# RWKV-style block on one core: the sums of the present token's part as column tiles of 64 tokens, and a new order of all engines

## The chip, the cores and the metric

One NeuronCore of one Trainium2 chip runs the whole program. The metric is the device time of one execution in microseconds; the kernel before was run three times, and their median is 341.69 us (340.33 to 343.31). The core has five engines that read their own instruction streams: TensorE (PE in the profile, PEld for its weight loads), VectorE (DVE), ScalarE (ACT), GpSimd (POOL) and SyncE (SP, which here issues all DMAs).

## The reference

Three layers follow one another, in float32, for 2 batches, 768 tokens and 384 = 8 x 48 channels:

```
for t in range(S):                                   # a linear attention with decay, per head (48 x 48 state)
    cur = einsum('bhd,bhe->bhde', u * k_t, v_t)
    y[t] = einsum('bhd,bhde->bhe', r_t, state + cur)
    state = w_t[..., None] * state + einsum('bhd,bhe->bhde', k_t, v_t)
h = gelu(x @ w_in); u, v = halves of h               # x is y, w_in 384 x 1024
v_s = w_sg @ layernorm(v) + b_sg                     # w_sg 768 x 768, over the tokens
x = x + (u * v_s) @ w_out
k = relu(mix(x, x_prev, mu_k) @ w_k) ** 2            # w_k 384 x 1024
out = sigmoid(mix(x, x_prev, mu_r) @ w_r) * (k @ w_v)
```

The part of `y[t]` that comes from `cur` is the present token's part: the number `sum_d r[t,d] u[d] k[t,d]` of each head and token, times `v_t`. The change concerns how TensorE forms this number.

## The kernel before

**The work.** Tokens are taken in four groups g of 384 (two batches, two halves), each in three chunks of 128. The attention is done in 16 units: unit i is one group and one pair of heads (p = 0 to 3), units 0 to 3 belong to group 0, 4 to 7 to group 1, and so on. The heads of a pair lie on partitions 0 to 47 and 64 to 111. The channels of r, k and w come in 12 packs (three for each group), pack j of a group holding pair j; the rows 48 to 63 and 112 to 127 of the three packs hold pair 3, and small DMAs (`move`) collect these into the tile `six`. The fifth to eighth layer steps use matrices of 64-bit input that DVE and ACT first turn into pairs of float32r (high and low part); each product of two such pairs is three TensorE products.

**The order.** Nothing is scheduled by a planner at run time. The string ORDER is read token by token, each token calls one method, and each engine keeps its instructions in the order in which the tokens stand. An engine that waits holds everything behind it. The tokens that matter here:

- for a pack: `L` load of the decays, `q` load of r and k, `D`, `j`, `g` the decay products and their inverses (DVE), `d` their product with r and k (DVE), `K` the product r x k that the sums read (DVE), `f` a range test (ACT), `6` the `move`;
- for a unit: `A` scores (TensorE, six products into the PSUM tile `pA`), `P` sums (TensorE, also into `pA`), `T` and `k` the turned keys (TensorE, ACT), `S`, `s`, `x` the states of the three chunks (TensorE, TensorE, ACT), `m` the mask on the scores and `n` the product of the sums with v (both DVE, both reading `pA`), `J`, `N`, `I` the output products (TensorE), `O` and `o` the copy and, for p = 3, the DMAs that share its rows out into `xT` (ACT, SP);
- for the layers: `C` with a number, the pieces of weights (`l` load, `x`, `b`, `t`, `o` on DVE, `h`, `r`, `q` on ACT); `X` the split of `xT` (ACT `h`, DVE `l`); `v`, `u` the products with w_in; `M` those with w_sg; `G`, `W` the gate and w_out; `H`, `Y`, `E`, `R`, `Z`, `z`, `y` the last layer;
- `e` a product that nobody reads (line 620), 128 x 512 in bfloat16, which keeps TensorE at work; `Q` the load of the constants; `|` the point where the attention's memory goes to the second half of the work.

A token such as `v0.2` or `M1.3` that stands several times runs one further step of the same piece of work each time: its first place is TensorE's.

**Rings that order the work.** `pA` has one buffer: the scores of a unit wait until `m` and `n` of the unit before have read it. The results of `v`, `u`, `M`, `W` and `E` take turns in three PSUM buffers (`ps_d`), so that the fourth of them waits until ACT or DVE has read the first. `wt` and `rk` have two buffers each. The pair that w_out is cast into lies in memory that the attention has until its last share DMA has landed.

**The lines that the change touches.** `sums` (line 319 on) is six products of a unit, each a chunk and a head: 48 rows, 128 tokens as the weights, and one moving column, a column of u. They write one column for each chunk into each of the two banks of `pA`, and `now` (line 361 on) reads them from there. The scores (line 317) have weights of the same 48 x 128 shape; the states (lines 334 and 345) have weights of 64 or 48 columns at column 0 or 64 of the array.

Of the kernel before, what the change touches and what calls it, by code (L numbers as in the profile page):

```python
# [36 lines left out]
ORDER = """e e L0 e q0 D0 j0 g0 f0 d0 e e e e e e e e e e e e e e e e e e e Q K0 A0 P0 L1 w0 q1 L2 D1 n0 j1 m0 g1 e e T0 e e e k0 S0.0 S0.1 J0 x0.0 s0.1 S0.2  # L37
x0.1 e N0 f1 s0.2 I0 x0.2 D2 d1 j2 K1 g2 A1 P1 w1 q2 C0.l m1 d2 n1 L3 K2 C0.x D3 T1 e e e e e f2 k1 S1.0 S1.1 x1.0 J1 s1.1 S1.2 A2 P2 x1.1 s1.2 x1.2
O0 e N1 T2 e I1 60 61 w2 L4 k2 S2.0 S2.1 O1 x2.0 m2 C0.b n2 j3 D4 g3 j4 62 A3 P3 q3 w3 q4 C1.l C0.t m3 g4 n3 s2.1 S2.2 J2 x2.1 s2.2 x2.2 e e T3 N2 J3
k3 C0.h S3.0 S3.1 e x3.0 N3 s3.1 S3.2 I2 K3 C0.o d3 C1.x x3.1 f3 I3 O3 s3.2 C1.r x3.2 f4 O2 C2.l w4 d4 C1.b A4 P4 m4 w5 L5 C2.x n4 e e T4 k4 C1.q e e  # L40
e S4.0 s4.0 S4.1 J4 o3 o3 o3 x4.0 s4.1 C1.t C1.h x4.1 K4 C2.b A5 P5 T5 N4 I4 k5 X0.2.h D5 C2.t X0.1.h S5.0 s5.0 S5.1 C2.h C2.r j5 X0.2.l C1.o C2.o e
v0.2 x5.0 X0.0.h C2.q C0.r s5.1 g5 X0.0.l C0.q x5.1 v0.0 q5 C3.l w6 C4.l 64 C5.l 63 C3.x d5 C3.b X0.1.l T6 v0.1 C3.t K5 65 m5 O4 k6 v0.0 f5 C3.h C3.r
C4.x n5 C3.o S6.0 s6.0 S6.1 J5 N5 I5 x6.0 C3.q s6.1 x6.1 C5.x C4.b C5.b C4.t C5.t A7 P7 T7 C4.h C4.o C5.h v0.2 C5.r L7 L6 C5.o u0.3 q6 w7 C11.l O5
u0.3 C11.h k7 D6 u0.2 u0.1 j6 g6 f6 m7 n7 A6 P6 d6 C11.o m6 n6 D7 K6 v0.2 v0.0 S7.0 s7.0 S7.1 J7 x7.0 s7.1 x7.1 J6 T8 N6 N7 A8 P8 I7 I6 q7 L8 C9.l w8
C7.l w9 j7 g7 m8 q8 D8 n8 j8 K8 d7 K7 g8 d8 v0.0 u0.1 k8 C5.q S8.0 S8.1 O7 v0.0 x8.0 O6 o7 o7 o7 J8 s8.1 S8.2 u0.0 C4.r f7 v0.1 x8.1 N8 I8 s8.2 C9.h
x8.2 A9 P9 u0.2 X1.1.h T9 X1.1.l m9 C7.h C7.o n9 C9.o X1.2.h X1.0.h X1.0.l k9 v1.1 S9.0 S9.1 x9.0 J9 s9.1 S9.2 A10 P10 x9.1 s9.2 v0.2 O8 u0.0 q11
C17.l C17.h L9 D9 X1.2.l v0.0 j9 g9 w10 68 v1.1 x9.2 f8 u1.2 v1.2 m10 T10 N9 v1.0 v0.1 v1.1 k10 v0.2 v0.2 v0.1 u1.2 w11 C6.l q9 66 d9 K9 L10 C8.l C8.h
C8.o n10 S10.0 S10.1 x10.0 f9 J10 s10.1 S10.2 I9 x10.1 s10.2 x10.2 67 A11 P11 T11 u1.1 N10 L11 C12.l q10 v1.2 O9 k11 v1.1 S11.0 S11.1 C6.h v0.1 x11.0
v1.1 C17.o D10 j10 m11 g10 n11 v0.1 C6.o d10 J11 s11.1 S11.2 A12 P12 x11.1 s11.2 C15.l D11 j11 g11 d11 C15.h x11.2 v1.0 u1.3 T12 u1.0 N11 I11 I10 v1.0
v1.2 C10.l w12 n12 m12 K10 C10.h C15.o v1.1 A13 P13 v1.0 C12.h B w13 n13 C10.o K11 m13 O11 k12 S12.0 s12.0 S12.1 u1.3 v1.0 v1.0 x12.0 u1.0 v1.2 u1.1  # L50
v1.2 J12 s12.1 o11 O10 o11 o11 C14.l C4.q x12.1 v1.2 M0.1 M0.3 T13 M0.3 C12.o M0.3 N12 M0.0 X2.1.h f11 C14.h k13 X2.1.l M0.1 M0.0 C13.l C13.h C14.o
C13.o M0.1 v2.1 S13.0 s13.0 S13.1 J13 x13.0 s13.1 x13.1 C16.l C16.h X2.2.h A14 P14 611 w14 69 C21.l X2.2.l C16.o w15 C18.l 610 N13 T14 M1.3 M0.0 C21.x
C21.b n14 C21.t m14 I13 I12 A15 P15 C20.l C21.r n15 M1.3 C20.x M1.3 m15 C26.l k14 v2.1 v2.1 v2.1 O13 S14.0 s14.0 S14.1 C21.q x14.0 J14 s14.1 x14.1
X2.0.h X2.0.l v2.2 T15 M1.0 O12 C26.r M1.0 C20.b C20.t k15 v2.2 C26.q S15.0 s15.0 S15.1 x15.0 J15 s15.1 v2.2 f10 v2.2 x15.1 C20.r C20.q N15 N14 M1.1
I14 I15 C19.l O15 o15 o15 C18.r O14 o15 | C20.h C21.h C18.q G0.3.h M1.0 M1.1 v2.0 C20.o C19.x C21.o C18.x C19.b C18.b G0.3.l C19.t M0.2 M1.2 v2.0
C19.r v2.0 C19.h v2.0 v2.0 v2.1 v2.2 M0.2 C19.o C26.x M0.2 C26.b C26.t v2.0 M1.2 v2.1 G0.0.h C19.q G0.2.h u2.0 u2.0 u2.3 u2.2 u2.1 v2.2 M1.1 C23.l
C27.l G0.1.h u2.3 G0.2.l G0.0.l C18.t C18.h C23.r C26.h G0.1.l C18.o C22.l u2.1 X3.0.h u2.2 X3.1.h X3.2.h W0.1 C23.x M1.2 C23.b X3.0.l C26.o C22.x
X3.2.l C22.b W0.1 C22.t X3.1.l C23.t W0.2 W0.2 W0.0 W0.0 C22.h C23.h C23.o C34.l v3.0 v3.0 v3.0 v3.1 v3.1 C23.q v3.0 C34.x C22.o v3.2 u3.2 v3.1 u3.1
v3.2 v3.2 v3.0 u3.2 u3.1 v3.2 u3.3 u3.0 C34.b C34.t v3.0 v3.2 v3.1 v3.1 v3.1 v3.2 C27.x C27.b C27.t G1.3.h u3.0 G1.0.h u3.3 C27.r C27.q C34.h M2.2
M3.1 M2.1 C27.h G1.2.h C34.r C34.q G1.1.h M2.2 G1.0.l C22.r C22.q G1.3.l G1.2.l C27.o C34.o G1.1.l C24.l M3.1 C24.x C24.b C24.r C24.t C24.q M2.2 W1.0  # L60
M2.1 C35.l C25.l C25.x C25.b C35.r C24.h C35.q C25.r C37.l C24.o W1.0 C35.x C35.b C35.t C35.h C25.q W1.1 M2.0 C38.l W1.1 C25.t C25.h C25.o C38.x M2.1
C37.r M2.3 M2.3 M2.3 M3.1 C35.o M2.0 W1.2 G2.1.h C37.q G2.2.h C37.x G2.1.l M2.0 G2.2.l C37.b W1.2 G2.3.h G2.0.h M3.2 M3.3 M3.0 M3.2 C37.t C38.b G2.3.l
M3.2 G2.0.l C38.t M3.3 C36.l C28.l W2.0 H0 Y0.0.0.a Y0.0.2.a Y0.0.0.b Y0.0.0.c Y0.0.1.a Y0.1.0.a Y0.1.1.a C36.r C37.h Y0.1.0.b Y0.1.1.b C36.q M3.0
M3.0 C37.o Y0.0.1.b C28.x W2.0 C38.h Y0.0.2.b C28.b W2.2 W2.1 C38.r C38.q Y0.0.2.c Y0.0.1.c Y0.1.0.c W2.1 Y0.1.2.a M3.3 E0.0 Y0.1.2.b E0.0 E0.2 E0.2
C28.r C38.o C36.x C36.b C28.t E0.0 E0.2 C36.t W2.2 Y0.1.1.c E0.1 E0.4 G3.0.h C28.h E0.0 E0.2 C36.h E0.2 C28.q E0.1 Y0.1.2.c C36.o C30.l C29.l C31.l
E0.5 R0.0 E0.3 R0.1 E0.0 C29.x C29.b C28.o E0.1 E0.1 E0.5 C31.x C31.b C29.t C29.h R0.0 G3.1.h E0.1 H1 C29.o C30.x G3.2.h C29.r C29.q E0.4 C30.b E0.5
C30.t C30.r C31.t Y1.0.0.a Y1.1.0.a C31.h Z0.0 E0.6 E0.5 C30.h Y1.0.1.a C30.o C32.l C32.x C31.o E0.5 C33.l E0.3 E0.4 E0.3 E0.4 E0.4 C32.b E0.3 C33.x
E0.3 C32.t C33.b C33.t C30.q E0.7 Z0.1 Z0.2 R0.2 C32.h E0.6 C32.o Y1.0.2.a E0.6 Y1.0.0.b E0.7 C31.r C33.h C33.o R0.2 E0.6 E0.7 E0.7 Y1.1.0.b Y1.0.1.b
Y1.1.1.a E0.6 Y1.1.1.b Y1.0.2.b R0.1 Y1.0.0.c E0.7 Z0.3 Z0.4 Z0.5 Z0.6 Y1.0.1.c Y1.0.2.c E1.1 Z0.7 Y1.1.2.a E1.1 Y1.1.2.b Y1.1.2.c E1.1 E1.0 E1.0 E1.0
# [826 lines left out]
```

## Time and profile before

| what | value |
|---|---|
| median of three runs | 341.69 us (340.33 to 343.31) |
| profiled execution | 341.91 us, span 340.1 us |
| PE busy, PEld busy | 330.4 us (97%), 306.2 us (90%) |
| DVE, ACT, POOL busy | 231.9 us (68%), 181.5 us (53%), 28.5 us (8%) |
| granted TensorE clock | 0.991 of full speed |
| chain that ended last | PE 80%, DVE 10%, ACT 5% |
| scores L317, sums L324 in that chain | 4%, 3% |

The busy times are shares of the span. A product is counted from its start to the end of its passage through the array, which is longer than the time until the next may start, so that a PE that is busy all the time is not a PE that starts something all the time; the distance between the starts of two weight loads says more. Instructions of DVE overlap a little as well: the next often starts some 80 ns before the one before it is over.

### The profile page before, as it was taken

The page shows a single profiled execution, that of the slowest core. Times are in us where ns is not written, and L with a number is a line of the kernel's source. Part 1 is how long each engine was busy: PE and PEld are TensorE (multiplying, and loading weights), DVE is VectorE, ACT ScalarE, POOL GpSimd, SP SyncE. Part 2 cuts the span into 40 slices and gives each one's busy share as a digit, 9 for nine tenths or more (in the row PEclk, how much of TensorE's full clock was granted, in tenths as well). Part 3 has the DMA queues.
Part 4 walks back from the last instruction along what each step waited for, and adds up shares of the span by engine and source line. Part 5 has one row for each costly group of instructions (what it writes and reads, how often), then busy time and mean ns, then how long its engine had stood idle before and what let it go on. Part 6 is the DMA issues. An engine that isn't in the chain of part 4 may idle for free.

```text
span 340.1 us, 6557 instructions
## 1 busy us (share of the span) xinstructions
PE 330.4 (97%) x2534; PEld 306.2 (90%) x2534; DVE 231.9 (68%) x427; ACT 181.5 (53%) x439; POOL 28.5 (8%) x74
## 2 busy tenths in 40 slices
...
GB/s 215 156 202 180 226 210 162 82 173 155 168 29 132 225 4 52 19 162 64 3 113 123 76 46 47 94 93 1 2 0 71 1 0 2 69 2 0 69 25 52
DMA packets 16500, 29.80 MB, mean 88 GB/s; under 512 B 2256, under 2 KB 12496, under 8 KB 16464
## 3 DMA queue, kind: packets, MB, share of 16 engines
...
q14 instruction: 15, 0.12, 0.1%
...
## 4 chain that ended last, share of the span: by engine, by line
PE 80%; DVE 10%; ACT 5%; issue 2%; DMA 1%; SPq 1%; POOL 1%; ACTq 0%; POOLq 0%; DVEq 0%
PE po L541 9%; PE pA L317 4%; PE idle L620 4%; PE pk L188 4%; PE pk L190 4%; PE pk L189 4%; PE ps L188 3%; PE ps L190 3%; PE ps L189 3%; PE py L374 3%; PE po L190 3%; PE po L188 3%; PE po L189 3%; PE py L384 3%; PE pv L188 3%; PE pA L324 3%
## 5 line engine op out<-in xcount | busy, mean ns | idle before, releaser
L188 PE MATMUL ps<-wsg,vn_hi 128*128 128x384 f32 x96 | 32.8, 342 | 0.0
L188 PE MATMUL pk<-xk_hi,wk_hi 128*128 128x384 f32 x96 | 32.5, 338 | 0.3 <-ACT kr L513 0.3
L190 PE MATMUL ps<-wsg,vn_lo 128*128 128x384 f32 x96 | 32.4, 337 | 0.0
L189 PE MATMUL ps<-wsg,vn_hi 128*128 128x384 f32 x96 | 32.4, 337 | 0.0
L189 PE MATMUL pk<-xk_lo,wk_hi 128*128 128x384 f32 x96 | 32.3, 337 | 0.0
L190 PE MATMUL pk<-xk_hi,wk_lo 128*128 128x384 f32 x96 | 32.3, 337 | 0.0
L513 ACT ACTIVATE kr<-pk 128x384 f32<-128x384 f32 x32 | 15.6, 489 | 29.9 <-PE pk L190 19.6
L515 DVE TENSOR_TENSOR kr<-kr 128x384 f32<-128x384 f32 x32 | 17.7, 555 | 14.0 <-ACT kr L513 14.0
L522 DVE TENSOR_TENSOR kk_lo<-kr,kk_hi 128x384 fp32r<-128x384 f32 x32 | 17.6, 554 | 13.2 <-ACT kk_hi L520 13.1
L520 ACT CAST kk_hi<-kr 128x384 fp32r<-128x384 f32 x32 | 16.1, 511 | 18.2 <-DVE kr L515 12.9
L541 PE MATMUL po<-pl_win_hi,kk_hi 128*128 128x384 f32 x81 | 23.0, 337 | 0.0
L188 PE MATMUL pu<-xs_hi,win_hi 128*128 128x384 f32 x48 | 16.9, 352 | 2.5 <-DVE sg L460 2.5
L460 DVE SCALAR_TENSOR_TENSOR sg<-ps,c_sb,bsg_bc 128x384 f32<-128x384 f32 x16 | 9.8, 614 | 13.9 <-PE ps L190 13.8
L541 PE MATMUL po<-pl_win_lo,kk_hi 128*128 128x384 f32 x63 | 18.5, 340 | 0.2 <-DVE pl_win_lo L169 0.2
L188 PEld LDWEIGHTS pk<-xk_hi,wk_hi 128*128 128x128 f32 x96 | 18.0, 188 | 0.6 <-ACT kr L513 0.6
L541 PE MATMUL po<-pl_win_hi,kk_lo 128*128 128x384 f32 x54 | 18.3, 338 | 0.0
L188 PEld LDWEIGHTS ps<-wsg,vn_hi 128*128 128x128 f32 x96 | 18.0, 188 | 0.1
L189 PEld LDWEIGHTS ps<-wsg,vn_hi 128*128 128x128 f32 x96 | 18.0, 188 | 0.0
L190 PEld LDWEIGHTS pk<-xk_hi,wk_lo 128*128 128x128 f32 x96 | 18.0, 188 | 0.0
L190 PEld LDWEIGHTS ps<-wsg,vn_lo 128*128 128x128 f32 x96 | 18.0, 188 | 0.0
L189 PEld LDWEIGHTS pk<-xk_lo,wk_hi 128*128 128x128 f32 x96 | 18.0, 188 | 0.0
L358 DVE TENSOR_TENSOR am<-pA,c_sb 128x768 f32<-128x768 f32 x16 | 15.2, 950 | 2.9 <-PE pA L324 2.9
...
## 6 DMA issues: line engine op xcount, KB each, us to landing
...
```

Of the source, the lines that this page charges most:

```text
L188: T.matmul(ps, lh, rh, start=(i == 0), stop=False)
L189: T.matmul(ps, lh, rl, start=False, stop=False)
L190: T.matmul(ps, ll, rh, start=False, stop=(i == n - 1))
L317: T.matmul(u.pA[:, h, c * C:(c + 1) * C], u.kinv[o:o + D, c, :], u.rp[o:o + D, c, :], start=True, stop=True)
L324: T.matmul(u.pA[:, h, TB + c:TB + c + 1], u.home()[o:o + D, 2 * WL + c * C:2 * WL + (c + 1) * C], c_sb[o:o + D, CU + u.p:CU + u.p + 1], st ...
L358: V.tensor_mul(u.am.rearrange("p h (c t) -> p h c t", c=NCB), u.pA[:, :, :TB].rearrange("p h (c t) -> p h c t", c=NCB), mask[:, None, None ...
L513: A.activation(kr, ps, AF.Relu)
L515: V.tensor_mul(kr, kr, kr)
L520: A.copy(hi, kr)
L522: V.tensor_sub(lo, kr, hi.bitcast(F32))
L541: T.matmul(pv[g][s], l, wv[i][r], start=st, stop=(i == KF - 1 and l is ll))
L620: T.matmul(ps_d.tile([P, 512], F32, name="idle", tag="d"), d[:, :P], d[:, :512], start=True, stop=True)
```

## The change

The sums take another shape. Each product still reads one chunk, but now half of its tokens (64 columns of the weights, at column 0 and at column 64 of the array), over all 112 rows of the two heads, and moves two columns: u of the first head and u of the second, each zero on the other head's rows. The result is one column for each head, in the first bank alone. The number of products stays at six. The two columns of the four pairs are made once, by four products on POOL behind the load of the constants. `now` reads the six columns from where they are.

The order of all engines is new; the multiset of tokens is the same, 1250 of them and 44 `e`. Ahead of the first unit stood 22 unread products and stand 19; 8 stand behind its sums, where 2 stood.

```diff
-ORDER = """e e L0 e q0 D0 j0 g0 f0 d0 e e e e e e e e e e e e e e e e e e e Q K0 A0 P0 L1 w0 q1 L2 D1 n0 j1 m0 g1 e e T0 e e e k0 S0.0 S0.1 J0 x0.0 s0.1 S0.2
...
-v0.2 x5.0 X0.0.h C2.q C0.r s5.1 g5 X0.0.l C0.q x5.1 v0.0 q5 C3.l w6 C4.l 64 C5.l 63 C3.x d5 C3.b X0.1.l T6 v0.1 C3.t K5 65 m5 O4 k6 v0.0 f5 C3.h C3.r
...
-C7.l w9 j7 g7 m8 q8 D8 n8 j8 K8 d7 K7 g8 d8 v0.0 u0.1 k8 C5.q S8.0 S8.1 O7 v0.0 x8.0 O6 o7 o7 o7 J8 s8.1 S8.2 u0.0 C4.r f7 v0.1 x8.1 N8 I8 s8.2 C9.h
-x8.2 A9 P9 u0.2 X1.1.h T9 X1.1.l m9 C7.h C7.o n9 C9.o X1.2.h X1.0.h X1.0.l k9 v1.1 S9.0 S9.1 x9.0 J9 s9.1 S9.2 A10 P10 x9.1 s9.2 v0.2 O8 u0.0 q11
...
+ORDER = """e e L0 D0 j0 g0 f0 e L1 D1 e e e e q0 K0 d0 e e e e e e e e Q q1 w0 j1 g1 d1 K1 e e e e T0 k0 A0 S0.0 S0.1 P0 e e e e e e e e f1 x0.0 n0 m0 A1 s0.1 P1
+S0.2 w1 L2 q2 J0 x0.1 s0.2 e e e x0.2 D2 j2 g2 m1 n1 d2 C1.l C1.x T1 k1 e e N0 S1.0 S1.1 x1.0 A2 s1.1 S1.2 J1 f2 x1.1 s1.2 x1.2 L3 K2 D3 P2 C1.b C0.l
...
+C5.q j7 g7 d7 K7 m8 J6 S8.1 N6 I6 L8 v0.2 f7 u0.1 x8.0 n8 A9 s8.1 S8.2 J8 x8.1 s8.2 P9 o7 q8 w9 C9.o D8 j8 g8 m9 K8 n9 x8.2 u0.3 d8 L9 O6 v0.0 v0.2
+v0.2 v0.0 C6.o C10.h D9 K9 u0.0 u0.2 o7 66 o7 f8 X1.0.h X1.0.l T9 A10 k9 S9.0 S9.1 x9.0 w10 C12.l C12.h J9 P10 s9.1 S9.2 N9 N8 x9.1 u0.2 v0.1 s9.2 I8
+I9 X1.1.h x9.2 C14.l B C12.o m10 j9 v1.0 C14.h u0.0 X1.2.h O8 g9 X1.1.l C10.o T10 k10 C14.o X1.2.l v1.2 u1.1 w11 q10 68 n10 C11.l 67 S10.0 S10.1 J10
...
+S15.1 J15 C15.h C15.o M0.2 n15 M0.2 x15.0 C21.r s15.1 x15.1 N15 I15 I14 C26.l C18.l v2.0 C21.q C19.r C19.q O15 O14 v2.2 o15 o15 o15 | C18.r C21.h
+C18.q C20.h v2.2 v2.0 C21.o v2.1 M1.1 C18.x C18.b C20.o C26.x C26.b M1.1 M1.1 C18.t v2.2 C18.h C18.o C19.x C19.b C26.t M0.1 C19.t M1.0 v2.0 v2.1 v2.1
+M1.0 M1.3 C26.h C26.o M1.3 M1.0 C19.h M1.2 M1.2 C19.o C23.l C22.l C26.r v2.1 G0.3.h C22.x C23.x u2.3 C26.q v2.0 v2.2 v2.2 v2.0 u2.3 v2.1 G0.1.h C22.b
...
+    uu = [ap1.tile([R, 2], F32, name=f"uu{p}") for p in range(NP)]
...
         def sums(u):
 
             for c in range(NCB):
-                for h in range(2):
-                    o = 64 * h
-                    T.matmul(u.pA[:, h, TB + c:TB + c + 1], u.home()[o:o + D, 2 * WL + c * C:2 * WL + (c + 1) * C],
-                             c_sb[o:o + D, CU + u.p:CU + u.p + 1], start=True, stop=True)
+                k = u.home()[:, 2 * WL + c * C:2 * WL + (c + 1) * C]
+                for o in (0, 64):
+                    T.matmul(u.pA[o:o + 64, 0, TB + 2 * c:TB + 2 * c + 2], k[:, o:o + 64], uu[u.p], start=True, stop=True)
...
-                         u.pA[:, :, TB:TB + NCB].rearrange("p h c -> p c h")[:, :, :, None].broadcast_to([P, NCB, 2, D]),
+                         u.pA[:, 0, TB:TB + 2 * NCB].rearrange("p (c h) -> p c h", c=NCB)[:, :, :, None].broadcast_to([P, NCB, 2, D]),
...
             nc.sync.dma_start(c_sb, cst)
+            for p in range(NP):
+                G.tensor_scalar_mul(uu[p], c_sb[:R, CB:CB + R:64], c_sb[:R, CU + p:CU + p + 1])
             G.tensor_scalar_mul(g_sb, g_sb, float(DH) ** 1.5)
```

## Rows read from the trace of the kernel before

**Rows 1.** Busy times by stretch: us, PE, PEld, DVE, ACT, POOL, PEclk, DMA.

```profile
8.72:65.38 56.66, 56.66 (x716) 47.28 (x715) 51.05 (x85) 35.26 (x94) 4.98 (x11) 1.00 0.62 179
...
152.00:335.30 183.30, 182.79 (x1033) 180.49 (x1033) 123.48 (x239) 90.14 (x204) 9.37 (x15) 1.00 0.14 45
```

**Rows 2.** Timeline of weight loads, scores, sums, states: start us, us, engine, line.

```profile
53.88 0.75 PEld L317 LDWEIGHTS pA<-pk 48*128 48x128 f32 x12 [0.25 <-issue]
54.55 0.75 PEld L324 LDWEIGHTS pA<-c_sb,pk 48*128 48x128 f32 x12
55.31 0.19 PEld L334 LDWEIGHTS pkv<-vk,kT 128*64 128x64 f32 x4
```

**Rows 3.** Timeline of weight loads, narrow groups of the states.

```profile
17.30 0.31 PEld L334 LDWEIGHTS pkv<-vk,kT 128*64 128x64 f32 x8 [0.42 <-ACT kT L310]
...
19.99 0.19 PEld L345 LDWEIGHTS pkv<-sx,c_sb 112*64 112x64 f32 x4
...
72.52 0.25 PEld L334 LDWEIGHTS pkv<-vk,kT 128*48 128x48 f32 x4
```

**Rows 4.** Timeline of weight loads, full-width loads behind column tiles.

```profile
57.24 0.30 PEld L306 LDWEIGHTS ptr<-c_sb,pk 112*128 112x128 f32 x3 [0.17 <-issue]
```

**Rows 5.** Timeline of the start, unread products and DVE's first wait for sums.

```profile
1.44 7.35 PE L620 MATMUL idle<-d1pat 128*128 128x512 bf16 x22 [1.44 <-POOL lim_tanh L119]
...
10.28 0.46 DVE L364 TENSOR_TENSOR vg<-pA,vk 128x288 f32<-128x288 f32 x1 [2.40 <-PE pA L324]
```

**Rows 6.** Groups of DVE by shape: busy us, mean ns, idle before.

```profile
L246 DVE TENSOR_TENSOR_SCAN pk<-wt,d1pat 128x387 f32<-128x387 f32 x12 | 11.4, 952 | 3.5 <-POOL xT L225 2.4 <-DMA wt<-in_wp_dram 1.1
L257 DVE TENSOR_TENSOR pk<-pk,rk 128x768 f32<-128x768 f32 x12 | 11.4, 952 | 0.1
...
L261 DVE TENSOR_TENSOR pk<-rk 128x384 f32<-128x384 f32 x12 | 6.6, 547 | 0.0
...
L169 DVE TENSOR_TENSOR wsg<-wsg_raw,wsg 128x384 fp32r<-128x384 f32 x12 | 6.5, 548 | 0.0
```

**Rows 7.** Timeline: DVE's `n8`, and the scores of unit 9.

```profile
61.63 0.43 DVE L364 TENSOR_TENSOR vg<-pA,vk 128x288 f32<-128x288 f32 x1
...
65.38 0.75 PEld L317 LDWEIGHTS pA<-pk 48*128 48x128 f32 x12
```

**Rows 8.** Timeline of weight loads: one `J`, one `u`, one `N`, one `I`.

```profile
61.40 0.68 PEld L374 LDWEIGHTS py<-am,vk 128*48 128x48 f32 x12
...
62.47 0.19 PEld L188 LDWEIGHTS pu<-xs_hi,win_hi 128*128 128x128 f32 x1
...
63.97 0.42 PEld L378 LDWEIGHTS py<-c_sb,vg 128*112 128x112 f32 x3
...
64.57 0.39 PEld L384 LDWEIGHTS py<-pk,sx 48*48 48x48 f32 x8 [0.17 <-issue]
```

**Rows 9.** Weight loads around two `v` groups, and one stretch's busy times.

```profile
67.72 0.21 PEld L188 LDWEIGHTS pv<-win_hi,xs_hi 128*128 128x128 f32 x1 [0.61 <-ACT xs_hi L415]
...
71.57 0.31 PEld L334 LDWEIGHTS pkv<-vk,kT 128*64 128x64 f32 x8 [0.44 <-issue]
...
78.77 0.19 PEld L188 LDWEIGHTS pv<-win_hi,xs_hi 128*128 128x128 f32 x1
...
81.06 0.31 PEld L334 LDWEIGHTS pkv<-vk,kT 128*64 128x64 f32 x8 [0.37 <-ACT uT L451]
...
69.00:70.00 1.00, 1.00 (x4) 0.71 (x3) 1.00 (x4) 0.25 (x1) 0.00 (x0) 0.50 1.03 326
```

**Rows 10.** Timeline behind the last shares: TensorE's and ACT's waits.

```profile
132.36 0.46 PEld L384 LDWEIGHTS py<-six,sx 48*48 48x48 f32 x8
...
138.76 0.93 ACT L166 CAST wout_hi<-wout_x 128x384 fp32r<-128x384 f32 x2 [3.75 <-DMA xT<-t]
...
143.63 0.19 PEld L188 LDWEIGHTS pu<-xs_hi,win_hi 128*128 128x128 f32 x1 [0.67 <-DVE sg L460]
...
147.62 0.19 PEld L188 LDWEIGHTS pu<-xs_hi,win_hi 128*128 128x128 f32 x1 [2.46 <-DVE sg L460]
```

More of the change, by code (lines that the diff above doesn't have):

```diff
@@ L49 @@
[L49 to L68, printed above, removed]
@@ new lines @@
+61 60 w2 C0.x C0.b j3 m2 g3 q3 62 N1 e e T2 I0 L4 n2 C1.t K3 d3 D4 I1 k2 O0 S2.0 S2.1 x2.0 J2 s2.1 S2.2 A3 f3 x2.1 s2.2 C1.h x2.2 P3 e T3 e N2 e w3 q4
+k3 S3.0 S3.1 O1 x3.0 C1.r m3 n3 K4 j4 g4 d4 A4 s3.1 S3.2 J3 x3.1 s3.2 C1.q x3.2 P4 C3.l L5 w5 w4 m4 D5 C0.t n4 N3 e T4 e e C2.l I3 k4 O3 I2 S4.0 s4.0
+S4.1 J4 x4.0 s4.1 O2 x4.1 C0.r C0.q j5 C1.o g5 e e e e T5 N4 q5 C2.x C2.b C2.t d5 o3 o3 o3 k5 C2.r C0.h C0.o A5 S5.0 s5.0 S5.1 P5 I4 X0.2.h x5.0 s5.1
+X0.0.h C2.h O4 f4 x5.1 X0.2.l 64 C5.l w6 K5 63 65 C2.o v0.2 C3.x X0.0.l T6 v0.0 k6 C2.q C3.r X0.1.h C3.q n5 m5 C5.x C5.b A7 C5.t X0.1.l S6.0 s6.0 S6.1
```

48 lines of the change are left out of this document (30 added, 18 removed).

## The prediction, made before the changed kernel was run

> **What bounds the kernel now.** I read the busy times by stretch first. Up to 65 us TensorE and DVE both work nearly without a pause: DVE is busy 51.05 of 56.66 us there, and from 152 us on TensorE starts 1033 products in 183.3 us, 0.177 us each, while DVE has a third of its time free [rows 1]. So there are two regimes. Late, a microsecond taken out of TensorE's stream is a microsecond of the end. Early, each unit's scores wait for DVE's `m` and `n` of the unit before, because `pA` has one buffer, so that DVE's stream sets the pace and what TensorE saves turns into waiting. The reader is to see in the timeline that even there a few waits stand out: DVE idles 2.40 us for the first sums, since 22 unread products, 7.35 us of them, stand before the first scores [rows 5]; a `v` group at 67.7 us waits and then runs at half the granted clock [rows 9]; and behind the attention's last shares ACT is held for 3.75 us and TensorE later for 0.67 and 2.46 us [rows 10].
>
> **The sums.** A unit's scores and sums are twelve weight loads each (two for a product) of 128 columns, and twelve such loads take 0.75 us from the first start to the last end [rows 2]. The new sums are twelve loads of 64 columns at alternating column halves, the shape of the states: four of these take 0.19 us, eight take 0.31, so four more cost 0.12 [rows 2, 3], and twelve should take 0.31 + 0.12 = 0.43. That is 0.32 us less for a unit, 5.1 us for sixteen. The shape itself (112 rows, two moving columns) isn't in the trace. Its bounds: a group of four that took 0.25 us [rows 3] gives 0.75 for twelve, no gain at all; at the least twelve take what four take, 0.19, a gain of 0.56 for a unit. A loss I exclude only as far as no row has a narrow load slower than a wide one. I take 0.32, the rows that are nearest in shape.
>
> A narrow group behind a wide one of the same rows starts without idle time [rows 2], but a full-width group behind column tiles waited 0.17 us [rows 4]. The sums now change array shape between themselves and the scores, which they did not before. The Trainium skill, TensorEngine Tiling (Array Packing), section Key Properties, says that a change of tiling mode drains TensorE, which speaks against the new shape; in the new order, though, all sixteen sums stand beside a group of states or `J`, which have their mode, and I count 71 changes of mode in place of 77, so by that rule the sum would be about 6 x 0.17 = 1.0 us better. I leave this out of the sum, since not every change shows a wait.
>
> **The head, up to the scores of unit 9.** Unread products are 44 before and after, and all of them stand ahead of `A9` in both orders, so they cancel there. The start changes: three fewer stand ahead of the first unit, and DVE is given `j1 g1 d1 K1` before it must wait for the first sums. I therefore take its 2.40 us of idling as gone. The second pack's load now stands ahead of the first `rk` and of the constants on SP, which delays these by one issue; DVE has `D1` to do meanwhile, so nothing. The four POOL products stand ahead of the gain's, long before the first sums: nothing. If SP or POOL were late after all, the first unit pays it once.
>
> In the new order `A9` stands right behind `n8`. Up to `n8`, DVE has the same instructions in both orders but for two: `d7` and `K7` have come in, `D8` and `C11.o` have gone out, 0.952 + 0.547 against 0.952 + 0.548 [rows 6]. So I put the new `n8` at the old one's end, 61.63 + 0.43 = 62.06, less 2.40: 59.7 us. The old scores of unit 9 start at 65.38 [rows 7]. The new ones come 5.7 us earlier, but with less done. By counting tokens, TensorE has put behind `A9` two `u` groups (1.50 each, from the first load to the next group's), `J8` (0.68), `N8` (0.42), `I8` (0.39) and three state groups (some 0.13 each): 4.9 us [rows 8]. The nine sums ahead of `A9` bring nothing of their own, as DVE sets that point. The seven behind it bring 7 x 0.32 = 2.2. Head and sums: 5.7 - 4.9 + 2.2 = **3.0 us**. For DVE's other idle time in the head I assume what it was: 56.66 - 51.05 - 2.40 = 3.2 us [rows 1, 5].
>
> **The event at 67 us.** The `v` group there waited 0.61 us for `X1.1.h`, which ACT could not start before a share's DMA had landed, and then nine products took 3.85 us up to the next group, against 2.29 for the group at 78.77; the granted clock was 0.50, the lower of its two levels [rows 9]. Together 0.61 + 1.56 = 2.2 us. In the new order the first share is issued a whole unit earlier (`o7` behind `P9`, `X1.0.h` after `u0.0 u0.2 o7 66 o7`), and `T9 A10 S9 J9 P10` and more stand between the splits and `v1.0`. I take the wait and the slow stretch as gone: **2.2 us**; the ends are 0 and 2.2. What could take its place: `A9`, which by the above may make TensorE wait for DVE.
>
> **Behind the last shares.** The old outer products end at about 132.8 and ACT gets on at 138.76, 5.9 us later [rows 10]. The new order has three groups for TensorE in between, `v2.1`, `M1.1`, `M1.0`: 45 products, 8.4 us by 0.2 and 0.177 each (an estimate from the 9 products in about 2 us of [rows 9] and from [rows 1]). Then `M1.3` needs the PSUM buffer of `v2.1`, whose GELU is ACT's ninth instruction behind the held cast: eight instructions of some 0.7 us make 5.9 + 5.9 = 11.8. So TensorE waits about 3.4 us, against 0.67 + 2.46 = 3.1 before [rows 10]. I take this as equal, with ends of -3 and +3.
>
> **The last layer** keeps its work, and TensorE was full there [rows 1]. I cost its new order at nothing; the cover is DVE's free third, and a `kk` or conversion that comes late would cost TensorE directly.
>
> **Sum.** 3.0 + 2.2 + 0 = 5.2 us. The profiled execution took 341.91 (span 340.1 and 1.8 around it), 0.2 above the median of 341.69: 336.7 against the former, **336.5** against the median.
>
> **Rivals.** (1) *The clock event only moves.* TensorE waits for DVE at `A9` or `A10`, and another group behind such a wait runs at the lower level. For it: the wait before the old event was only 0.61 us. Against: many small groups fill that stretch. Then 2.2 are lost: 338.7. (2) *The sums are no cheaper*, the shape costs what the old one did, by the group of four in 0.25 us: 7 x 0.32 is lost, again 338.7. (3) *DVE and TensorE wait for each other in the head*: DVE comes to `m` with the scores not yet done, unit by unit, and nine times pays scores and sums, 0.67 + 0.43 = 1.1 us: +9.9, 346.4, slower. It decides at `n8`: each microsecond after 59.7 costs one, from 64.9 on nothing is gained, from 68.3 on the kernel is over 1% slower. For it: 25 unread products now stand among the units, where 22 stood, so the order expects waits there. Against: DVE has conversions between `A` and `m` of most units. (4) *DVE's remaining idle time in the head shrinks too*: up to 3.2 us more, 333.3.
>
> **How the numbers follow.** Forecast 0.48, (1) 0.15, (2) 0.08, (3) 0.12, (4) 0.17. What a measurement can tell from no change is about 1%, 3.4 us, so faster means under 338.3. The forecast's own scatter is some 3 us, by the two ends of the wait behind the shares, and puts 0.06 of its chance above that line; of (1), 0.03 falls under it. Faster 0.42 + 0.17 + 0.03 = 0.62, slower 0.12, the rest 0.26. The range runs from 331.0 (case 4 with a cheaper sum or a shorter wait at the shares: 333.3 - 2.3) to 341.5 (case 1 or 2 with a longer one: 338.7 + 2.8); it leaves out case 3 and the tails of the others.
>
> **What would show it.** The twelve loads of the sums on line 325 in about 0.43 us; no DVE wait of over a microsecond for the first sums; `n8` at about 59.7 and the scores of unit 9 right behind it; full granted clock between 60 and 75 us; one wait of about 3 us for TensorE some 8 us after the last outer products, and from there to the end the same 0.177 us for each product. The prediction is wrong if `n8` comes after 62, if the loads of the sums take over 0.6 us, if the clock falls somewhere in the head, or if the last layer shows waits of TensorE that add up to more than 2 us.

## The result and the profile after

The changed kernel took 338.6 us (median of 11 executions, 337.8 to 340.1) against 342.4 for the kernel before beside it: ratio 0.989, 95% interval 0.986 to 0.992, so about 3.7 us or 1.1% faster. Measured again with other kernels it was 338.8, ratio 0.991 (0.988 to 0.995). The forecast was 336.5, a gain of 5.2. The profiled execution has a span of 337.0 us (before 340.1). One execution further down, of the new sums in the old order, ran over 1% slower than the others of its kernel, at a lower granted clock, and its time and profile are not used.

The head first. Weight loads and VectorE's (DVE's) products of the kernel after, timeline: start us, us, engine, line.

```profile
10.26 0.45 DVE L364 TENSOR_TENSOR vg<-pA,vk 128x288 f32<-128x288 f32 x1
...
59.16 0.46 DVE L364 TENSOR_TENSOR vg<-pA,vk 128x288 f32<-128x288 f32 x1
...
59.84 0.75 PEld L318 LDWEIGHTS pA<-pk 48*128 48x128 f32 x12 [0.18 <-DVE vg L364]
...
91.73 0.43 PEld L325 LDWEIGHTS pA<-uu,pk 112*64 112x64 f32 x12
92.08 0.20 PEld L334 LDWEIGHTS pkv<-vk,kT 128*64 128x64 f32 x4
```

The twelve loads of the sums take 0.43 us and the next group starts 0.35 us after the first of them, where it was 0.76 [rows 2]. DVE's 2.40 us of waiting at 10 us are gone [rows 5]. `n8` ends at 59.62 instead of 62.06, and unit 9's scores start at 59.84 instead of 65.38 [rows 7].

Next the waits of TensorE and what holds them, kernel after, timeline of the weight loads, ScalarE (ACT) and SyncE's queue (SPq).

```profile
36.62 0.51 ACT L415 CAST xs_hi<-xT 128x384 fp32r<-128x384 f32 x1 [2.11 <-DMA xT<-t]
37.39 0.19 PEld L345 LDWEIGHTS pkv<-sx,c_sb 112*64 112x64 f32 x4 [2.26 <-ACT sx L353]
...
61.95 1.22 SPq L273 DMA_DIRECT2D six<-pk  x2
63.28 1.31 SPq L395 DMA_DIRECT2D xT<-t  x1
...
66.77 0.52 ACT L415 CAST xs_hi<-xT 128x384 fp32r<-128x384 f32 x1 [1.69 <-DMA xT<-t]
67.67 0.31 PEld L334 LDWEIGHTS pkv<-vk,kT 128*64 128x64 f32 x8 [1.16 <-ACT kT L311]
...
70.07 0.19 PEld L345 LDWEIGHTS pkv<-sx,c_sb 112*64 112x64 f32 x4 [0.17 <-ACT uT L451]
...
71.33 0.19 PEld L188 LDWEIGHTS pv<-win_hi,xs_hi 128*128 128x128 f32 x1 [0.18 <-ACT sl L353]
```

At 67 us a split of `x` still waits for a share's DMA, and TensorE stands for 1.16 us where it was 0.61 [rows 9]. The clock stays at full speed there. It falls elsewhere. Behind the last shares, kernel after, timeline and then busy times by stretch (us, PE, PEld, DVE, ACT, POOL, granted clock as a share of full speed, DMA share, GB/s).

```profile
130.01 0.51 ACT L166 CAST wout_hi<-wout_x 128x384 fp32r<-128x384 f32 x1 [3.17 <-DMA xT<-t]
133.74 0.61 DVE L460 SCALAR_TENSOR_TENSOR sg<-ps,c_sb,bsg_bc 128x384 f32<-128x384 f32 x1
134.41 0.19 PEld L188 LDWEIGHTS ps<-wsg,vn_hi 128*128 128x128 f32 x1 [2.54 <-DVE sg L460]
...
136.58 0.58 ACT L429 ACTIVATE v<-pv 128x512 f32<-128x512 f32 x1
...
148.47 0.19 PEld L188 LDWEIGHTS po<-ga_hi,wout_hi 128*128 128x128 f32 x1
```

```profile
135.00:136.00 1.00, 1.00 (x5) 1.00 (x4) 0.42 (x2) 0.55 (x2) 0.54 (x1) 0.50 0.00 0
...
148.47:332.20 183.73, 183.66 (x1037) 181.44 (x1036) 122.00 (x237) 90.63 (x204) 5.56 (x15) 1.00 0.13 42
```

The wait of 2.54 us is shorter than the two of before together (0.67 + 2.46) [rows 10], but from 135.0 to 138.4 the clock is at its lower level (granted 0.50 of full speed), and ten loads come 0.32 us apart instead of 0.177: some 1.5 to 1.7 us. The outputs `W` start at 148.47; in the kernel before they start here:

```profile
151.26 0.19 PEld L188 LDWEIGHTS po<-ga_hi,wout_hi 128*128 128x128 f32 x1 [0.53 <-issue]
```

From there on 1037 products take 183.7 us, 0.177 each, as before [rows 1].

So a lead of 5.5 us at unit 9's scores is 2.8 at the outputs and 3.1 at the end.

### The profile page after: what moved, and what is told of

Read it like the earlier page. It is cut to its first block, busy times and chain, and to the rows that moved or that the text cites. A ratio compares the mean times of both kernels' runs of the same rounds, so it can differ in the third digit from the quotient of the medians.

```text
span 337.0 us, 6538 instructions
## 1 busy us (share of the span) xinstructions
PE 324.3 (96%) x2529; PEld 302.9 (90%) x2534; DVE 232.0 (69%) x427; ACT 182.1 (54%) x439; POOL 29.3 (9%) x78
## 4 chain that ended last, share of the span: by engine, by line
PE 80%; DVE 9%; ACT 4%; DMA 3%; issue 2%; SPq 1%; ACTq 0%; DVEq 0%
PE po L541 11%; PE pk L189 5%; PE pk L190 5%; PE pk L188 5%; PE ps L188 4%; PE ps L190 4%; PE ps L189 4%; PE po L190 3%; PE po L189 3%; PE po L188 3%; PE py L374 3%; PE pA L318 3%; PE pu L188 2%; PE pu L190 2%; PE pu L189 2%
## 5 line engine op out<-in xcount | busy, mean ns | idle before, releaser
L188 PE MATMUL ps<-wsg,vn_hi 128*128 128x384 f32 x96 | 33.3, 347 | 2.2 <-DVE sg L460 2.2
L190 PE MATMUL ps<-wsg,vn_lo 128*128 128x384 f32 x96 | 33.1, 344 | 0.0
L189 PE MATMUL ps<-wsg,vn_hi 128*128 128x384 f32 x96 | 33.0, 344 | 0.0
L188 PEld LDWEIGHTS ps<-wsg,vn_hi 128*128 128x128 f32 x96 | 18.5, 192 | 2.6 <-DVE sg L460 2.5
L189 PEld LDWEIGHTS ps<-wsg,vn_hi 128*128 128x128 f32 x96 | 18.6, 194 | 0.0
L190 PE MATMUL po<-ga_hi,wout_lo 128*128 128x384 f32 x48 | 16.2, 337 | 0.0
```

What stands on the lines that cost most here:

```text
L188: T.matmul(ps, lh, rh, start=(i == 0), stop=False)
L189: T.matmul(ps, lh, rl, start=False, stop=False)
L190: T.matmul(ps, ll, rh, start=False, stop=(i == n - 1))
```

## The experiments

All ratios are to the kernel before on the same chip, with 95% intervals. Since each execution lists its mean granted clock, I also give a **time at full clock**, an estimate: the mean over executions of (time - 340 us x (1 - mean clock)). It scatters by 0.3 to 1.0 us. The mean clock also counts the lower level behind TensorE's last product, which costs its stream nothing: in the profile of before it stands from 337.5 us to the end at 340.1, in that of after for the last 0.6 us. So the column takes off up to 1.3 us too much, and a difference in it of less than a microsecond says little.

| kernel | median us | ratio | mean clock | at full clock |
|---|---|---|---|---|
| before (25 executions) | 341.6 | 1 | 0.994 | 339.3 |
| after | 338.6 | 0.989 (0.986-0.992) | 0.992 | 336.1 |
| new sums, old order | 339.6 | 0.996 (0.994-0.997) | 0.994 | 337.8 |
| old sums, new order | 343.6 | 1.007 (1.004-1.010) | 0.989 | 340.1 |
| after, units 0 to 8 with old sums | 341.5 | 1.001 (0.999-1.004) | 0.993 | 339.2 |
| after, gap at 132 us filled | 338.6 | 0.991 (0.987-0.995) | 0.993 | 336.2 |
| after, third share first | 337.3 | 0.986 (0.982-0.989) | 0.995 | 335.3 |
| the same, both gaps filled | 337.4 | 0.987 (0.984-0.990) | 0.999 | 336.7 |
| after, GELU of `v2.1` early | 338.3 | 0.989 (0.986-0.992) | 0.995 | 336.3 |
| after, splits late | 339.6 | 0.993 (0.991-0.996) | 0.989 | 336.0 |
| share, GELU and splits together | 338.2 | 0.991 (0.988-0.993) | 0.994 | 336.1 |
| share, GELU and DVE's order | 341.5 | 0.999 (0.996-1.001) | 0.985 | 336.3 |

**Shape and order apart.** The new sums in the old order, and the old sums in the new order:

```diff
 (after)  -ORDER = """<new>"""    +ORDER = """<old>"""
 (before) -ORDER = """<old>"""    +ORDER = """<new>"""
```

> The sums in column tiles, all else in the order of before. Theory: the shape alone is worth what it shortens where TensorE sets the pace, the seven units from 9 on; a group of sums goes from 0.75 us to 0.43, so 7 x 0.32 = 2.2 us, and the groups ahead of unit 9 bring nothing, since VectorE sets the pace there: 342.4 - 2.2 = 340.2 us (339.4 to 341.2), with the 2.4 us wait of VectorE at 10 us, the wait of 0.61 at 67 us and the stretch at half clock still there. Rival 1: the shorter loads bring nothing, because the next groups wait for something else: 342.4. Rival 2: the shape is all of the gain, the order none: 338.6.

> The order of after, with the sums in the shape of before. Theory: the order is worth the rest, 3.8 - 2.2 = 1.6 us, from VectorE's first wait and the last unit of the first share, less what the slow stretch at 135 us takes: 340.8 us (340.0 to 341.6); unit 9's scores start within 0.4 us of where they do in the kernel after (59.84). Rival 1: the two parts need each other, the order alone gives nothing or loses: 342.4 or more. Rival 2: the order is all of it: 338.6.

The shape alone is worth 1.5 us (0.9 to 2.2), in the forecast's direction. The order alone is 2.4 us *slower* (1.5 to 3.3), where a gain of 1.6 was expected; both together gain 3.7. So the parts don't add, and the rival that they need each other holds. The weight loads show why: one unit's scores (48x128), states (`pkv`) and sums, first with the old sums in the new order, then in the kernel after, then with the new sums in the old order.

```profile
17.10 0.75 PEld L317 LDWEIGHTS pA<-pk 48*128 48x128 f32 x12
17.97 0.19 PEld L345 LDWEIGHTS pkv<-sx,c_sb 112*64 112x64 f32 x4
...
18.81 0.24 PEld L345 LDWEIGHTS pkv<-sx,c_sb 112*64 112x64 f32 x4
19.10 0.75 PEld L324 LDWEIGHTS pA<-c_sb,pk 48*128 48x128 f32 x12
19.87 0.29 PEld L378 LDWEIGHTS py<-c_sb,vg 128*112 128x112 f32 x3
```

```profile
17.89 0.24 PEld L345 LDWEIGHTS pkv<-sx,c_sb 112*64 112x64 f32 x4
18.01 0.47 PEld L325 LDWEIGHTS pA<-uu,pk 112*64 112x64 f32 x12
18.50 0.30 PEld L378 LDWEIGHTS py<-c_sb,vg 128*112 128x112 f32 x3
```

```profile
53.04 0.75 PEld L318 LDWEIGHTS pA<-pk 48*128 48x128 f32 x12 [0.25 <-issue]
53.91 0.43 PEld L325 LDWEIGHTS pA<-uu,pk 112*64 112x64 f32 x12
54.25 0.20 PEld L334 LDWEIGHTS pkv<-vk,kT 128*64 128x64 f32 x4
```

Scores take 0.87 us from start to start where a group of column tiles follows, and took 0.67 where sums of their own shape followed [rows 2]; the old sums start 0.29 us after four loads of the states, the new ones 0.12; and the group behind the new sums starts after 0.49 us where it is wide (18.01 to 18.50), after 0.35 where it is narrow (91.73 to 92.08, above). A change from wide to narrow loads or back costs between 0.14 and 0.20 us, then. The Trainium skill, TensorEngine Tiling (Array Packing), section Key Properties, says that a change of tiling mode drains TensorE; these rows agree in so far as each change costs time, and no row shows the drain itself. In the new order states stand between scores and sums, and a state group with sums, with a wide group behind it, takes 1.06 us with the old shape (18.81 to 19.87) and 0.61 with the new (17.89 to 18.50): 0.45 saved. In the old order scores and sums stand together, 1.43 us before [rows 2] and 1.21 now: 0.22 saved, since the change between them is new. Old sums in the new order also pay for more changes: counted as the forecast counted them, 87 in all where the kernel before has 77 and the kernel after 71. Ten more at some 0.2 us are 2 us (an estimate), near the 2.4 us that the order alone lost.

The next kernel says where the time lies.

**Old sums in the head only.**

```diff
 (and the matching read by DVE)
+                if u.i <= 8:   # 24 products of one column, as before
+                    for h in range(2):
+                        o = 64 * h
+                        T.matmul(u.pA[:, h, TB + c:TB + c + 1], u.home()[o:o + D, ...], c_sb[...])
+                    continue
                 for o in (0, 64):
```

> The kernel after, with the sums of units 0 to 8 in the old shape (24 products of one column each) and those of units 9 to 15 in the new. Theory: up to unit 9 VectorE sets the pace, so nine groups that are 0.32 us longer on TensorE cost nothing: 338.6 us (338.0 to 339.4), n8 on VectorE at 59.2 within 0.4 and unit 9's scores right behind it. Rival 1: they lie on the path also there: 9 x 0.32 = 2.9, 341.5. Rival 2: only the first of them is on it (the first product of VectorE waits for it): 338.9 to 339.2.

It took 341.5 us, 2.9 more than the kernel after (3.4 to 4.1 by the ratios, 1.001 for 0.991 and 0.989): rival 1. Its price of 0.32 us for a unit was too low, though, and the lead is not all kept: `n8` starts 3.7 us later than in the second profile of the kernel after (59.75), which also had a fall of the clock near 40 us, and nine units at the 0.45 us above would be 4.1 (an estimate).

```profile
63.43 0.46 DVE L370 TENSOR_TENSOR vg<-pA,vk 128x288 f32<-128x288 f32 x1 [0.52 <-PE py L385]
```

What paces the head is read from DVE's waits up to 62 us, grouped (waiting line, releaser: us in total, times, longest), first in the kernel before, then in this one, then in the kernel after.

```profile
DVE vg L364 <- PE pA L324: 2.4, 1, 2.4
DVE am L358 <- PE pA L324: 2.4, 5, 0.7
```

```profile
DVE am L364 <- PE pA L327: 1.9, 5, 0.6
```

```profile
DVE xs_lo L417 <- ACT xs_hi L415: 1.9, 1, 1.9
...
DVE vg L364 <- PE py L378: 0.6, 1, 0.6
```

In the kernel before DVE waited five times, 2.4 us in all, for a unit's scores and sums on TensorE; with the old sums in the new order it does so again (1.9), with the new sums in the new order not once. From 8.5 to 30 us DVE is busy for 19.10 of 21.50 us before, for 19.59 with the old sums in the head, and in the kernel after for 21.29:

```profile
8.50:30.00 21.50, 20.97 (x321) 16.94 (x323) 21.29 (x34) 10.39 (x30) 3.12 (x9) 1.00 0.77 225
```

So the pace of the head changes hands with the sums: with the old ones TensorE holds DVE up, with the new ones DVE runs almost without a pause there. The seven later units are worth the difference between this kernel and the old sums throughout: 2.0 us by the medians, 0.9 at full clock.

The shape alone was run once more for a profile.

> The new sums in the old order, once more, for a profile without disturbance. Theory: units 9 to 15 gain 0.3 us each on TensorE but lose it at waits that are new there: 1.59 us for ScalarE's state at 82 us, as in the disturbed profile, stands again (1.2 to 1.8), and the time is 339.7. Rival: that wait was the disturbance's, it is gone, and the 2 us show up in waits behind the last shares, at 143 and 147 us, longer than 0.68 and 2.46 by as much.

One execution, 338.2 us, at full clock throughout (one of the earlier ones, also at 1.000, took 339.7). The wait at 82 us isn't there. The rival's longer waits aren't there either; weight loads, timeline:

```profile
139.52 0.19 PEld L188 LDWEIGHTS pu<-xs_hi,win_hi 128*128 128x128 f32 x1 [0.69 <-DVE sg L460]
143.51 0.19 PEld L188 LDWEIGHTS pu<-xs_hi,win_hi 128*128 128x128 f32 x1 [2.47 <-DVE sg L460]
```

Neither account held. By the rows above a unit saves less there, 0.22 us at most, so the seven units bring 1.5 at most in place of 2.2 (an estimate). And the nine units ahead bring something in the old order too, against the expectation: `n8` starts at 60.56 us, 1.07 earlier than before [rows 7], and DVE waits three times for scores and sums up to 62 us, 1.6 us in all, instead of five times.

**The half clock and the standstills.**

```diff
-... C19.t M1.0 v2.0 v2.1 v2.1 M1.0 M1.3 ...
+... C19.t M1.0 i i i i i i i i i i i v2.0 v2.1 v2.1 M1.0 M1.3 ...   # i: 512 unread columns
```

> The kernel after, with 11 more products of 512 columns, which nobody reads, on TensorE between M1.0 and M1.3, where it stands for 2.54 us from 131.9 to 134.4. Theory: the half clock of 135.1 to 138.3 follows from that standstill, so with TensorE kept busy the clock stays at 1.00 there, the loads of M1.3 come 0.177 us apart from the first on, and 338.6 - 1.7 = 336.9 us (336.3 to 337.6). Rival 1: the fall has another cause and comes anyway: 338.6, loads 0.32 apart. Rival 2: the clock stays, but what follows is bound by VectorE's backlog of conversions and gives it back: 338.0 to 338.8 with a clock of 1.00. Rival 3: the extra products end later than the wait did: 339 or more.

> The kernel after once more, unchanged, on the chip of the next kernels. Theory: 0.989 of before as first measured, and a second profile in which the same waits stand at the same places (2.0 to 2.3 us at 37, 1.16 at 67, 2.54 at 134), while the half clock may follow another of them than the one at 134 us, since the five profiles so far of kernels with these waits put it behind 37 us in three and behind 134 in two. Rival: the half clock belongs to the wait at 134 and stands there again, and only there.

The first theory was half right. Busy times by stretch, filled kernel, then the kernel after a second time:

```profile
39.00:40.00 1.00, 1.00 (x4) 0.81 (x3) 1.00 (x4) 0.49 (x3) 0.00 (x0) 0.50 0.93 281
135.00:136.00 1.00, 1.00 (x7) 0.68 (x6) 0.97 (x3) 0.73 (x1) 0.81 (x3) 1.00 0.00 0
```

```profile
39.00:40.00 1.00, 1.00 (x3) 0.72 (x3) 1.00 (x3) 0.38 (x3) 0.00 (x0) 0.50 0.97 328
137.00:138.00 1.00, 1.00 (x5) 1.00 (x5) 0.93 (x3) 1.00 (x3) 0.00 (x0) 0.50 0.68 139
```

With TensorE kept busy the clock stayed up at 135 us, but in that execution it fell at 38 us, behind the wait for the first shares, where the first profile of after had full clock. The kernel after, unchanged, fell at both places in its second profile. So where the clock falls isn't a property of the kernel alone, and the median didn't move (338.6). Then both standstills were filled, with the third share first:

```diff
-P5 I4 X0.2.h x5.0       ... o7 66 o7 f8       (and the eleven i as above)
+P5 I4 e e e e e e e e e X0.2.h x5.0   ... o7 o7 66 f8
```

> The third share first, and products that nobody reads in the two longest standstills of TensorE: 9 of 512 columns at 35 us and 11 at 132 us. Theory: the time is that of the full clock plus some 2 us for each fall of the clock, and each fall follows a standstill, so with both filled it comes out where the share-first kernel does at a clock of 1.00 (its one such run is 335.1): 335.6 us (335.0 to 336.5), and mean clocks of 0.996 and over in most runs. Rival 1: the standstills have nothing to do with the falls: 337.3 as the share-first kernel, with mean clocks from 0.986 to 1.0. Rival 2: with those two filled, the fall moves to the next standstill, 0.6 us at 68 us or 0.4 us at 150: 337.0 to 337.5.

All six executions had mean clocks of 0.997 to 1.000. A fall like that of 135.0 to 138.4 takes 0.005 off the mean, so none of them had one while TensorE had work; every other kernel that was run more than once has executions with a fall. Standstill and fall belong together, then, though a standstill alone isn't enough for one. The time was 337.4 all the same, where the theory had 335.6: by the last column it is 1.3 us worse than without the fillers. What costs that isn't shown; by the intervals it equals the third share first alone.

**The share behind a move.**

```diff
-u0.0 u0.2 o7 66 o7 f8 X1.0.h
+u0.0 u0.2 o7 o7 66 f8 X1.0.h
```

> The kernel after, with the third share of o7 on SyncE's queue ahead of the move 66 (1.22 us of issue). Theory: the split of the next part's first token chunk needs all three shares, and the third is issued behind that move; 1.2 us earlier takes away the wait of 1.16 us at 67.7 us: 337.4 to 337.8. Rival 1: TensorE's wait there hides VectorE's, which is full from 50 to 67 us, and nothing is won: 338.6. Rival 2: the move 66 then comes late for unit 9's rows and TensorE waits there instead: 339 or more.

The time was as expected, 337.3 us, 1.3 less than after; the intervals of the two ratios overlap. The wait is 0.62 in place of 1.16, but the stretch around it is no shorter. Timeline of the weight loads and one cast of ACT:

```profile
60.68 0.75 PEld L318 LDWEIGHTS pA<-pk 48*128 48x128 f32 x12 [0.18 <-DVE vg L364]
...
67.98 0.31 PEld L334 LDWEIGHTS pkv<-vk,kT 128*64 128x64 f32 x8 [0.62 <-ACT kT L311]
...
70.07 0.51 ACT L166 CAST wsg<-wsg_raw 128x384 fp32r<-128x384 f32 x1 [1.31 <-DMA wsg_raw<-in_w_sgT_dram]
...
70.84 0.19 PEld L345 LDWEIGHTS pkv<-sx,c_sb 112*64 112x64 f32 x4 [0.64 <-ACT sx L353]
...
72.09 0.19 PEld L188 LDWEIGHTS pv<-win_hi,xs_hi 128*128 128x128 f32 x1 [0.18 <-issue]
...
135.32 0.19 PEld L188 LDWEIGHTS ps<-wsg,vn_hi 128*128 128x128 f32 x1 [2.54 <-DVE sg L460]
```

The move and the loads behind it on the queue now come later: ACT waits 1.31 us for a weight, and the state `sx` behind that cast holds TensorE for 0.64 us where the wait was 0.17. So from unit 9's scores to the first products of `v1.0` it takes 11.41 us (60.68 to 72.09), and in the kernel after 11.49 (59.84 to 71.33). Over all profiles of kernels with both changes that stretch is 11.3 to 11.7 us with the share in its old place and 11.0 to 11.7 with the share first. The kernel has the lowest median of the study, but its mean clock is also higher, 0.995 for 0.992, which is some 0.9 us of the 1.3; that the pair of tokens made it faster isn't shown. Here the same 2.54 us at 135 had no fall behind it.

**Behind the last shares.**

```diff
-O14 v2.2 o15 o15 o15 | C18.r C21.h ... C21.o v2.1 M1.1 ... v2.0 v2.1 v2.1
+O14 v2.2 o15 o15 o15 | v2.1 C18.r v2.1 C21.h ... C21.o M1.1 ... v2.0 v2.1
-        ln = w2.tile([P, 4], F32, ..., tag="ln")
+        ln = w2.tile([P, 4], F32, ..., tag="ln", bufs=3)
```

> The kernel after, with the third token chunk's product v2.1 and its GELU on ScalarE ahead of C21's held cast (and a third small buffer for its sums). Theory: M1.3 takes the PSUM buffer that is freed first in program order, which in the kernel after is M1.1's, freed by VectorE at 134.35; with v2.1's freed earlier, at about 127, M1.3 starts right behind M1.0 at 131.9 and the 2.54 us wait and the half clock behind it go: up to 2.54 + 1.7 = 4.2 us at that point, and 1 to 3 us at the end, because VectorE's conversions behind it keep their times: 336.6 us (335.5 to 338). Rival 1: M1.3 waits for M1.1's buffer whatever v2.1 does: 338.6, the wait still 2.5. Rival 2: the wait goes to the next product, M1.2, or to the outputs W0: 338 to 338.6.

The wait of `M1.3` is gone, so it takes the buffer freed first in program order, and the theory of the buffer holds. The time is rival 2's, 338.3, with new waits at the next products. Weight loads, then DVE, timeline:

```profile
139.90 0.19 PEld L188 LDWEIGHTS pu<-xs_hi,win_hi 128*128 128x128 f32 x1 [1.44 <-DVE sg L460]
147.20 0.19 PEld L188 LDWEIGHTS po<-ga_hi,wout_hi 128*128 128x128 f32 x1 [1.11 <-issue]
```

```profile
130.86 0.56 DVE L169 TENSOR_TENSOR wout_lo<-wout_x,wout_hi 128x384 fp32r<-128x384 f32 x1 [9.40 <-ACT wout_hi L166]
```

DVE stands for 9.4 us behind ACT's held cast, as in the kernel after, and for 1.6 us at 144 us for a weight's DMA, so TensorE only waits one product later. Two further edits brought nothing. The splits of the first part placed late:

```diff
-P5 I4 X0.2.h x5.0 s5.1 X0.0.h C2.h O4 f4 x5.1 X0.2.l 64 C5.l w6 K5 63 65 C2.o v0.2 C3.x X0.0.l T6 v0.0 k6 ... n5 m5
+P5 I4 x5.0 s5.1 C2.h O4 f4 x5.1 64 C5.l w6 K5 63 65 n5 m5 T6 k6 X0.2.h X0.0.h X0.2.l C2.o v0.2 C3.x X0.0.l v0.0 ...
```

> The kernel after, with the splits of x of the first part (X0.2, X0.0) placed behind x5.1, n5, m5, T6 and k6 on every engine, where before they held ScalarE 2.11 us and VectorE 1.89 us until the first shares landed at 36.6 us. Theory: VectorE sets the pace up to unit 9, so its 1.89 us come back: n8 at 57.3 instead of 59.16, TensorE's wait of 2.26 at 37.4 under 0.6, and 338.6 - 1.8 = 336.8 us (336.0 to 337.6). Rival 1: the products v0.2 and v0.0 then come late and the wait moves to their GELUs: 338.6. Rival 2: VectorE gains at 37 us and loses it to the weights' chunks that arrive by DMA (it waits for winu at 41.4): 338 to 338.6.

> The three edits together (GELU of v2.1 early, third share first, splits late). Theory: they lie in different stretches and add: 2.0 + 1.0 + 1.8, so 333.8 us (332.5 to 335.5). Rival: what the first two stretches win, the outputs W0 and the conversions on VectorE from 140 us on give back, as they don't start earlier: 336 to 337.

The one wait of 2.26 became two, with the clock down behind them; weight loads, then busy times of the kernel with the splits late:

```profile
36.76 0.36 PEld L307 LDWEIGHTS ptr<-c_sb,pk 112*128 112x128 f32 x3 [1.25 <-ACT sx L353]
38.47 0.29 PEld L188 LDWEIGHTS pv<-win_hi,xs_hi 128*128 128x128 f32 x1 [1.35 <-ACT xs_hi L415]
```

```profile
39.00:40.00 1.00, 1.00 (x4) 0.74 (x3) 1.00 (x4) 0.97 (x3) 0.00 (x0) 0.50 0.86 261
```

339.6 us, where 336.8 was expected: `n8` starts at 61.40 us instead of 57.3. At full clock it equals the kernel after; its six executions have mean clocks of 0.986 to 0.993. The three edits together, 338.2 for an expected 333.8, don't add, though the profiled execution had no fall of the clock. Last, on top of the share and the GELU, DVE's two operations of `M1.1` and `M1.0` ahead of the conversions, and the chunks that wait for DMA behind the gates:

```diff
-C21.o M1.1 C18.x C18.b C20.o C26.x C26.b C18.t ...   G0.3.h C22.x C23.x u2.3 ... G0.1.h C22.b v2.1 ... G0.3.l
+M1.1 M1.0 M1.1 M1.1 C21.o C18.x C18.b C20.o C26.x C26.b M1.0 M1.0 C18.t ...   G0.3.h u2.3 ... v2.1 ... G0.3.l C22.x C23.x C22.b
```

> The third share first, the GELU of v2.1 early, and VectorE's order behind the last shares changed: M1.1's and M1.0's two operations ahead of the conversions that wait for the shares and for the weights, the first steps of the chunks C22 and C23 (1.60 us of wait for their DMA) behind the gates' low parts. Theory: with these TensorE waits at none of 134, 140 and 147 us for more than 0.5 us, the outputs W0 start 2 to 3 us earlier than the share-first kernel's 147.85, and 337.3 - 2.0 = 335.3 us (334.3 to 336.5). Rival: the outputs come earlier, but the next weights are converted later by as much and TensorE waits for those in the last layer: 337 or more, with a new wait between 150 and 230 us.

A miss on both theories: 341.5 us. DVE, then the weight loads:

```profile
134.07 0.62 DVE L460 SCALAR_TENSOR_TENSOR sg<-ps,c_sb,bsg_bc 128x384 f32<-128x384 f32 x1 [11.94 <-ACT vj L433]
```

```profile
144.84 0.29 PEld L188 LDWEIGHTS pu<-xs_hi,win_hi 128*128 128x128 f32 x1 [4.11 <-DVE sg L460]
```

`M1.1`'s first operation writes the small buffer `sg`, which it shares with the squares `vj` on ACT, and those stand behind the held cast. Moved ahead, it held DVE for 11.94 us until the squares were done, and all conversions after it.

## Why the prediction was right, and where it was not

**The sums** came out as sized in their loads, 0.43 us. What a unit saves was taken as 0.32 throughout; it is 0.45 where states stand ahead of the sums and 0.22 where the scores do. The changes of array shape, which the forecast counted (71 for 77) and left out of the sum as some 1.0 us, are worth 0.14 to 0.20 each and tie the shape to the order. The rival that the sums are no cheaper is out.

**The head** ended where the forecast put it: `n8` at 59.62 for 59.7, unit 9's scores right behind it, 5.5 us ahead for 5.7. (One profile: in others of kernels with the same head `n8` ends between 58.7 and 60.5.) But two sentences of that step fell. "The nine sums ahead of `A9` bring nothing of their own, as DVE sets that point" is wrong: they bring 2.9 us at the end and 3.7 at `n8`, as the kernel with old sums in the head showed. DVE seemed to pace the head because it was busy for 51 of 57 us [rows 1]; 2.4 us of its idle time were five waits for scores and sums, which the view of DVE's waits lists and the argument had left in "what it was". And the new order doesn't give 2.40 by itself: with the old sums it loses 2.4, with ten changes of shape more, and it takes new waits into the head (2.26 us of TensorE and 1.89 of DVE at 37 us, for the first shares). The terms were wrong, and that their sum was right is luck: 4.8 us of DVE's waits for scores and sums went (2.40 and 2.4), and about half of that was lost again, 1.6 us of it to longer waits for the shares and for `py`. The third rival, the two engines waiting for each other unit by unit, is what the new order does with the old sums, at 2 to 3 us instead of 9.9.

**The event at 67 us** is the step that failed, at 2.2 us. "The first share is issued a whole unit earlier" was true and beside the point: `X1.0.h` splits a token chunk over all three of the part's column groups, so it needs all three shares. The first was issued 3.5 us earlier than before (57.67 for 61.18), the third only 0.5 us, at 63.28 behind the move 66. In the kernel before, timeline of SyncE's queue:

```profile
63.76 1.40 SPq L395 DMA_DIRECT2D xT<-t  x1
```

The wait stayed, 1.16 us; moving that share up halved it, and the rest of it came back as a wait for what the share had overtaken on the queue. The clock's fall went from 67 us to behind the wait at 134 us, in the second profile to 37 and 135 us, which the forecast itself had named as a sign of being wrong ("if the clock falls somewhere in the head"). Over all executions the mean clock is 0.992 after and 0.992 to 0.994 before, so the clock costs about as much as it did. That is rival 1, "the clock event only moves", with another place than it named; 338.7 was its price, 338.6 was measured, and so close a match is partly luck. The chance of 0.15 was argued from many small groups in that stretch, and didn't ask where else TensorE stands.

**Behind the last shares** one wait instead of two was right, 2.54 us for a forecast 3.4, against 3.1 before. The releaser was wrong: the GELU of `v2.1` runs at 136.58, after `M1.3` has begun at 134.41; the buffer was `M1.1`'s, freed by DVE. The sum of that step was off as well: eight instructions of some 0.7 us are 5.6 us and not 5.9, which makes the forecast wait 3.1. The early GELU agrees with the rule of the buffers and brought no gain, with DVE held by ACT's cast as before.

**The last layer** kept its time: from the outputs to the end 188.8 us before and 188.5 after. In the experiments it took 187.8 where the outputs started at 152 or later and about 189.0 in four of five where they started near 147, so part of an earlier lead seems to be given back there; the tie is loose (188.0 for a start at 149.3, 188.8 for one at 146.1), and its cause stays open.

In sum: 3.0 (head and sums) came, 2.2 (the event) did not, and 338.6 is what is left. The old order has falls of the clock too, with the old sums and with the new, so a part of the difference between any two of these kernels, up to some 2 us in one execution, is the clock's.
